# Backward start of an attention and MLP block: a V tile and a dK tile exchanged, the rows of e released by an earlier add, dw4 stored in two parts

## The chip, the cores and the metric

The kernel runs on one core of one Trainium2 chip. The metric is the device time of one execution in microseconds (us), lower is better. Engines are named as in the profile: PE is TensorE, PEld its weight loads, DVE is VectorE, ACT is ScalarE, POOL is GpSimd and SP is SyncE; SP and POOL here mostly issue transfers, SP the loads and POOL the stores.

## The reference

One decode step of an adaptive-layernorm block and its gradients. The sizes are D = 640, 32 heads, 8192 cached positions, 192 columns per head, F = 1536, all arrays bf16.

```python
mod = (silu(c) @ w_mod).reshape(1, 6, 1, -1)          # sa, ca, ga, sb, cb, gb
h = layernorm(x) * (1 + ca) + sa
q = (h @ wq)                                          # 32 heads of 192
p = softmax(q K^T * 192 ** -0.5)                      # K: 32 x 8192 x 192
x = x + ga * ((p V) @ wo)
h = layernorm(x) * (1 + cb) + sb
x1 = h + shift_mix(h)                                 # one position: the mixed part is zero
out = x + gb * (x1 + gelu(layernorm(x1) @ w3) @ w4)
# returned: out and its gradients for x, K, V, wq, wo, w3, w4, c, w_mod
```

The large arrays are K and V, each 32 x 8192 x 192 numbers. Both are read, and dK and dV of the same size are written. For one head, dV is the outer product of the row of probabilities with do (the gradient of that head's output), and dK is the outer product of the column dS with q, where dS = p * (V do - correction). V is therefore read a second time in the backward part, to form V do.

## The kernel before, in words

**Tiles.** A head's K or V is handled in two halves of 128 partitions x 32 rows x 192 columns, 1536 KB each. Five such tiles, `KB0` to `KB4`, hold halves of K in the forward part; three, `VB[0]` to `VB[2]`, hold halves of V. Lines 353 and 354 give the five KB tiles names by their use at the end of the forward part, and the order `OB` in which the backward part uses them for its outputs:

```python
KX, KY, KC, KD, KE = (KB[(2 * HQ + k) % NKB] for k in (-4, -5, -3, -2, -1))
OB = (KC, KY, KX, KE, KD)
```

So KX is KB0, KC is KB1, KD is KB2, KE is KB3 and KY is KB4.

**The forward loop** (lines 516 to 600) goes over heads 0 to 30; the last head is finished by straight-line code from line 605 on. The last half of V goes to KY (line 665). KX then takes rows 4 to 11 of w4 (`load_rows`, lines 730 and 765), and KC takes part of the transposed w3 and of the transposed wo.

**The middle** (lines 731 to 975) finishes the attention output, runs the MLP forward and its gradients, and ends in `dao`, the gradient of the attention output. The pieces that the change names are these:
- `mp_out` (line 443) copies head 30's sums from PSUM on ACT, the second copy to the tile `mt`; `m_add` (line 456) adds that tile to a half of PSUM on DVE. Before, they stand at lines 910 and 954.
- `dw4_dve` (line 877) and `dw4_act` (line 912) each make some of the 12 row blocks of the gradient of w4, 128 x 640 per block, on DVE or ACT; `dw4_store` (line 881) issues their store on POOL. Before, blocks 0 and 1 are made at line 933, ahead of the product `pr` (line 935) that leads to `dao_bf` (line 952); blocks 2 and 3 follow at line 955, with a store of four blocks from KX. Blocks 4 to 8 go to KX too (lines 1353 to 1355), blocks 9 to 11 to the staging tile `stg0` (lines 1356 and 1357), each with a store of its own.
- `dx1_out` and `d_sb_out` (lines 958 and 968) are small vector computations, kept together with that of `du` in the list `late0` (line 1362).

**The backward loop** (line 1363) has 64 steps. Step s works on half `ht(s)`: step 0 on the second half of head 31 (V in KY), step 1 on its first half (V in `VB[2]`), steps 2 and 3 on head 30 (V in `VB[0]` and `VB[1]`), and so on downwards. For each half,
- `mul_q(s, 0)` and `mul_q(s, 1)` (line 1036) multiply V by do on DVE, a half of the half at a time; `tree_q` (line 1051) sums the products over the columns on PE with an identity matrix, into the one PSUM tile `dot_ps`; `dot_sum` (line 343) finishes the sum on DVE, as `dP`;
- `dv_groups` (line 1058) forms dV: PE multiplies a row of e (tile `er_b`, loaded by `load_er` from a scratch array in DRAM) with do into `dv_ps`, and ACT copies the result into the dV tile;
- `dk_part` (line 1070) forms dK on DVE from q and dS;
- `dv_store` and `dk_store` (lines 1316 and 1320) issue the stores on POOL; `load_v` (line 324) issues the load of the V half four steps on, on SP.

The start of step 0 is written out ahead of the loop (lines 1324 to 1362). The list `OL` gives dV and dK of successive steps the tiles of `OB` in turn: dV of step 0 KC, dK of step 0 KY, dV of step 1 KX, dK of step 1 KE, dV of step 2 KD, dK of step 2 KC, dV of step 3 KY. `v_buf(s)` gives the tile of V: KY for step 0, `VB[2]`, `VB[0]`, `VB[1]` for steps 1 to 3, and then these three in turn. V of step 4 thus goes to `VB[2]`, and its load, issued within step 0 (line 1407), waits for `mul_q(1, 1)`.

**What sets the order.** Within the forward and the backward part the program order is kept on PE, DVE, ACT and SP; POOL's stores are issued in program order too. A transfer into a tile waits for the last reader of the tile, and a write to a tile waits for the stores that read it. The pools of the backward part (`bst`, from line 982) lie over space that the forward part's pools held, and what is placed there waits for the last use of what lay there before: the two loads of `er_b` on line 1029 wait for the add in `m_add` that reads `mt`, and for the last matmul of line 919.

Besides the halves, `slot()` (line 1282) hands out side work (gradients of wo, wq, w3, w_mod and the output vectors) over the steps, by a count of slots that does not depend on time.

Of the kernel before, what the change touches and what calls it, by code (L numbers as in the profile page):

```python
# [20 lines left out]
def kernel(  # L21
# [28 lines left out]
    D = A_x.shape[-1]  # L50
# [66 lines left out]
    def tcol(n, name, dtype=FP32):  # L117
        return tmp.tile([P, n], dtype, name=name)
# [7 lines left out]
    def mean_sum(ps, groups, name):  # L126
        m = tcol(groups, name)
        V_.reduce_sum(out=m, in_=ps[:, 0 : groups * ND].rearrange("p (a b) -> p a b", b=ND), axis=AX.X)
        return m
# [187 lines left out]
    def flat(kb):  # L317
        return kb.rearrange("p j d -> p (j d)")


    NVB = 3
    VB = [vp.tile([P, JH, DH], BF16, name=f"VB{b}") for b in range(NVB)]

    def load_v(h, t, v):
        nc.sync.dma_start(out=v, in_=V_hd[h][:, t * JH : (t + 1) * JH, :])
        return v
# [24 lines left out]
    H1 = HQ - 1  # L351
    TL = NT - 1
    KX, KY, KC, KD, KE = (KB[(2 * HQ + k) % NKB] for k in (-4, -5, -3, -2, -1))
    OB = (KC, KY, KX, KE, KD)
    NVA = (7 * JQ) // 16
    MO = 256
    with tc.tile_pool(name="vs", bufs=3) as vsp, tc.tile_pool(name="ft", bufs=2) as ft, \
# [85 lines left out]
        def mp_out(h, mp):  # L443
            A_.copy(out=M1[:, h, :], in_=mp[:, 0:MW])
            mt = ft.tile([P, MW], FP32, name="mt", bufs=1)
            A_.copy(out=mt[64:128, :], in_=mp[64:128, MO : MO + MW])
            return mt

        def m_out(h, mp, op, os_):
            mt = mp_out(h, mp)  # L450
            o, z_h = os_head(h, os_)
            A_.copy(out=o, in_=op[:, 0:DH])
            A_.copy(out=z_h, in_=op[:, DH:MW])
            return mt

        def m_add(h, mp, mt):
            t, b = divmod(h, 2)
            V_.tensor_tensor(out=M2[64 * b : 64 * b + 64, t, :], in0=mp[0:64, MO : MO + MW], in1=mt[64:128, :], op=ALU.add)
# [56 lines left out]
        with tc.manual_schedule(engines=ORDER):  # L515
            for i in range(H1):
# [34 lines left out]
                if z is not None:  # L551
                    mt = m_out(i - 2, z["mp"], z["op"], os_)
# [124 lines left out]
            mt = m_out(H1 - 2, z["mp"], z["op"], os_)  # L677
# [15 lines left out]
            mp = psM.tile([P, 512], FP32, name="mp")  # L693
# [119 lines left out]
            def w3t(n=1):  # L813
                for _ in range(n):
                    next(w3t_it, None)
# [56 lines left out]
            w3t()  # L872
            pe.pop(0)()
            w3t()
            dw4_v = out_7.rearrange("(a p) r -> p a r", p=P)

            def dw4_dve(dst, a0, lo, hi):
                for a in range(lo, hi):
                    V_.tensor_scalar(out=dst[:, (a - a0) * D : (a - a0 + 1) * D], in0=dbo_bc, scalar1=g_[:, a : a + 1], scalar2=None, op0=ALU.mult)

            def dw4_store(dst, lo, n):
                nc.gpsimd.dma_start(out=dw4_v[:, lo : lo + n, :], in_=dst[:, 0 : n * D].rearrange("p (a r) -> p a r", a=n))
# [24 lines left out]
                    T_.matmul(h2_ps[:, k : k + 1], lhsT=w4r(a)[:, k * P : (k + 1) * P], rhs=g_bf[:, a : a + 1], start=(a == 0), stop=(a == NF - 1))  # L907
            do_t(TL, 0)
            do_t(TL, 8)
            mt = mp_out(H1 - 1, mp)  # L910

            def dw4_act(dst, a0, lo, hi):
                for a in range(lo, hi):
                    A_.activation(out=dst[:, (a - a0) * D : (a - a0 + 1) * D], in_=dbo_bc, func=ACT.Copy, scale=g_[:, a : a + 1])

            dn_ps = psO.tile([P, 256], FP32, name="dn_ps", tag="op")[:, 0:ND]
            for k in range(ND):
                for a in range(NF):
                    T_.matmul(dn_ps[:, k : k + 1], lhsT=w3T(a, k), rhs=du_bf[:, a : a + 1], start=(a == 0), stop=(a == NF - 1))

            sk = mean_sum(ps5, 5, "sk")
            w6 = col(6 * ND, "w6").rearrange("p (a b) -> p a b", b=ND)
            A1, Ag, B1, Bg, uu, vv = (w6[:, k, :] for k in range(6))
# [6 lines left out]
            NWg = col(4 * ND, "NWg").rearrange("p (a b) -> p a b", b=ND)  # L930
            V_.tensor_scalar(out=NW, in0=NW, scalar1=rho[:, 0:1], scalar2=None, op0=ALU.mult)
            V_.tensor_copy(out=bo, in_=h2_ps[:, 0:ND])
            dw4_dve(flat(KX), 0, 0, 2)
            pr = col(4 * ND, "pr").rearrange("p (a b) -> p a b", b=ND)
            V_.tensor_tensor(out=pr, in0=dn_ps[:, None, :].to_broadcast([P, 4, ND]), in1=G, op=ALU.mult)
            ps = mean_mm(pr.rearrange("p a b -> p (a b)"), 4 * ND)
# [14 lines left out]
            V_.reduce_sum(out=qr, in_=q4.rearrange("p a b -> p b a"), axis=AX.X)  # L951
            V_.tensor_tensor(out=dao_bf, in0=vg, in1=qr, op=ALU.add)
            V_.tensor_copy(out=d_n2, in_=dn_ps)
            m_add(H1 - 1, mp, mt)
            dw4_dve(flat(KX), 0, 2, 4)
            dw4_store(flat(KX), 0, 4)

            def dx1_out():
                q = pr
# [28 lines left out]
    NS = 2 * HQ  # L988
# [9 lines left out]
    def ht(s):  # L998

        return H1 - s // 2, (1 - s % 2 if s < 2 else s % 2)  # L1000
# [7 lines left out]
    stg0 = bst.tile([P, ND * CW], BF16, name="stg")  # L1008
# [38 lines left out]
    def half_q(s, q):  # L1047
        if halved(s, q):
            V_.tensor_tensor(out=pq[:, q, :, 0:HW], in0=pq[:, q, :, 0:HW], in1=pq[:, q, :, HW:DH], op=ALU.add)
# [8 lines left out]
    def dv_groups(dV, er, doh, gs):  # L1058

        dV4 = dV.rearrange("p (r k) d -> p r (k d)", r=4)  # L1060
        for g in gs:
            m, q = divmod(g, 2)
            ps = psV.tile([P, 2, 512], FP32, name="dv_ps", tag="v")
            for k in range(2):
                for b in range(2):
                    p0 = 32 * (2 * q + b)
                    T_.matmul(ps[:, b, k * DH : (k + 1) * DH], lhsT=er[p0 : p0 + 1, 2 * m + k, :], rhs=doh[p0 : p0 + 1, :], start=True, stop=True)  # L1067
            A_.copy(out=dV4[:, 2 * q : 2 * q + 2, m * PW : (m + 1) * PW], in_=ps[:, :, 0:PW])  # L1068
# [219 lines left out]
            prog[1] += 1  # L1288

    def v_buf(s):  # L1290
        return KY if s == 0 else VB[(s + 1) % NVB]

    OL = [OB[i % 5] for i in range(2 * NS - 5)]
    OL += [v_buf(NS - 3), OB[3], v_buf(NS - 2), OB[4], v_buf(NS - 1)]
    v_l = {s: v_buf(s) for s in range(4)}
# [27 lines left out]

    dV0 = OB[0]
    er = er_l.pop(0)
# [5 lines left out]
    do_mm(TL, 0)  # L1331
    mul_q(0, 1)
    half_q(0, 1)
    dv_groups(dV0, er, doh, (4,))
    tree_q(ps, 0, 0, 0, 6)
    dv_groups(dV0, er, doh, (6,))
# [13 lines left out]
    T_.matmul(c_ps, lhsT=c32, rhs=cs, start=True, stop=True)  # L1350
    dv_groups(dV0, er, doh, (5, 7))
    dv_store(0, dV0, JQ, JH)
    dw4_dve(flat(KX)[:, 4 * D :], 4, 4, 7)
    dw4_act(flat(KX)[:, 4 * D :], 4, 7, 9)
    dw4_store(flat(KX)[:, 4 * D :], 4, 5)
    dw4_act(stg0[:, 2 * D :], 9, 9, 12)
    dw4_store(stg0[:, 2 * D :], 9, 3)
    V_.scalar_tensor_tensor(out=cpr, in0=c_ps, scalar=32.0, in1=rinv, op0=ALU.mult, op1=ALU.mult)
    V_.memset(dha, 0.0)
    V_.memset(dsc, 0.0)  # L1360
# [1 line left out]
    late0 = [lambda: V_.scalar_tensor_tensor(out=du, in0=t_, scalar=-1.0, in1=d_g, op0=ALU.mult, op1=ALU.mult), dx1_out, d_sb_out]  # L1362
    for s in range(NS):
        h, t = ht(s)
        nxt = s + 1 < NS
        doh = do_of(h)
        qh = qs_bc[:, h * DH : (h + 1) * DH]
        dP = tcol(JH, "dP")
        dot_sum(ps, dP)
        dS4 = bst.tile([P, JH, 4], BF16, name="dS4", bufs=2)  # L1370
        V_.scalar_tensor_tensor(
            out=dS4,
            in0=dP[:, :, None].to_broadcast([P, JH, 4]),
            scalar=cpr[:, h : h + 1],
            in1=E_all[:, h, t * JH : (t + 1) * JH, None].to_broadcast([P, JH, 4]),
            op0=ALU.subtract,
            op1=ALU.mult,
        )
        dV, dK = OL[2 * s], OL[2 * s + 1]
        gs = [0, 1, 2, 3, 4, 5, 6, 7]  # L1380
        if not nxt:
            gs = [0, 2, 4, 6, 1, 3, 5, 7]
        if s == 0:
            gs = [None] * 8
        else:
            er = er_l.pop(s)
        if nxt:
            ps = psR.tile([P, JH, TS], FP32, name="dot_ps")

        def dv(k):  # L1390
            if gs[k] is not None:
                dv_groups(dV, er, doh, (gs[k],))

        def tree(q, lo, hi):
            if nxt:
                tree_q(ps, s + 1, q, lo, hi)

        dv(0)
        dv(1)
        slot()  # L1400
        tree(0, 0, 4)
        if nxt:
            mul_q(s + 1, 1)
            half_q(s + 1, 1)
            v_l.pop(s + 1, None)
        if s + 4 < NS:
            v_l[s + 4] = load_v(*ht(s + 4), v_buf(s + 4))
        dv(2)
        tree(0, 4, 8)
        dv(3)  # L1410
        tree(0, 8, 12)
        if row is not None:
            dq_cols(row)
            row = None
        dk_part(dK, qh, dS4, 0, JQ)
        if not nxt:
            dv_store(s, dV, 0, JQ, nc.sync)
            dk_store(s, dK, 0, JQ)
        slot()
        dv(4)  # L1420
        tree(1, 0, 3)
        dk_part(dK, qh, dS4, JQ, JH)
        while late0:
            late0.pop(0)()
        dk_store(s, dK, 0 if nxt else JQ, JH)
        dv(5)
        tree(1, 3, 6)
        slot()
        dv(6)
        tree(1, 6, 9)  # L1430
        dv(7)
        if s + 2 < NS:
            er_l[s + 2] = load_er(s + 2)
        if s == 0:
            pass
        elif nxt:
            dv_store(s, dV, 0, JH)
        else:
            dv_store(s, dV, JQ, JH, nc.sync)
        tree(1, 9, 12)  # L1440
        if h == H1:
            row = dq_rows(t, (KD, KE)[t], dS4)
        if s + 2 < NS:
            assert (s + 2) // 4 in done
            mul_q(s + 2, 0)
            half_q(s + 2, 0)
        done_s[0] = s + 1
        slot()
# [33 lines left out]
```

## Time and profile before

| what | us |
|---|---|
| three runs | 1411.46, 1413.57, 1414.79 |
| median | 1413.57 |
| the profiled execution | 1412.54 |
| its span, from the first to the last instruction | 1410.8 |
| busy in the span: PE | 1182.7 |
| DVE | 1112.0 |
| ACT | 902.5 |
| POOL | 106.0 |

1.74 us of the profiled execution lie outside its span. It moved 569.36 MB in its transfers, 404 GB/s over the span. The loads of V and K and the stores of dV and dK are 1536 KB each: 64 loads of K, 123 loads of V under that name (and more under others), 123 stores from the KB tiles. In the profile's pages, a line of the timeline gives the start in us, the busy time, engine, source line, operation, what is written and read, and, in brackets, the engine's idle time before it and what ended it. A line of the table of windows gives, for a stretch of the span, its length, the busy time of PE, PEld, DVE, ACT and POOL with the number of instructions in parentheses, the clock granted to PE as a share of full speed, the mean busy share of the core's 16 DMA engines, and the GB/s that they moved. That share is of packets in flight and can pass 1 by a little.

### The profile page before, as it was taken

The page shows a single profiled execution, that of the slowest core. Times are in us where ns is not written, and L with a number is a line of the kernel's source. Part 1 is how long each engine was busy: PE and PEld are TensorE (multiplying, and loading weights), DVE is VectorE, ACT ScalarE, POOL GpSimd, SP SyncE. Part 2 cuts the span into 40 slices and gives each one's busy share as a digit, 9 for nine tenths or more (in the row PEclk, how much of TensorE's full clock was granted, in tenths as well). Part 3 has the DMA queues.
Part 4 walks back from the last instruction along what each step waited for, and adds up shares of the span by engine and source line. Part 5 has one row for each costly group of instructions (what it writes and reads, how often), then busy time and mean ns, then how long its engine had stood idle before and what let it go on. Part 6 is the DMA issues. An engine that isn't in the chain of part 4 may idle for free.

```text
span 1410.8 us, 30413 instructions
## 1 busy us (share of the span) xinstructions
PE 1182.7 (84%) x12680; PEld 745.5 (53%) x12680; DVE 1112.0 (79%) x1461; ACT 902.5 (64%) x1971; POOL 106.0 (8%) x191
## 2 busy tenths in 40 slices
PE   3988989999998999797867998896877799878965
PEld 2777777777777778443323444443443344334421
DVE  4989999999999998886755875776775777868765
ACT  0767777777777778565545666665655476546654
POOL 0000000000000000110100111101110111101110
PEclk7899999999999999665555555556556555555555
DMA  9999999999999997599999999999999999999998
GB/s 375 389 398 419 418 416 423 411 422 417 418 415 415 408 416 291 209 365 427 424 388 424 427 422 426 421 425 425 425 421 425 414 413 426 419 404 396 424 369 373
DMA packets 76200, 569.36 MB, mean 404 GB/s; under 512 B 7294, under 2 KB 25038, under 8 KB 35998
## 3 DMA queue, kind: packets, MB, share of 16 engines
q1 hardware_dynamic: 51162, 342.03, 59.4%
q0 software_dynamic: 24384, 224.87, 38.3%
q8 instruction: 99, 1.62, 0.4%
q10 hardware_dynamic: 516, 0.51, 0.1%
q14 instruction: 39, 0.32, 0.1%
HBM read 340.95 MB, written 226.43 MB: 402 GB/s over the span
## 4 chain that ended last, share of the span: by engine, by line
issue 58%; DMA 17%; PE 9%; DVE 9%; POOL 5%; ACT 1%; SPq 0%; POOLq 0%; DVEq 0%; ACTq 0%
DMA KB<-in_A_k_cache_dram 7%; DVE prod L330 4%; DMA out_dram<-KB 3%; DMA w_st<-in_A_wq_dram 3%; PE mp L402 2%; DVE prod L334 2%; PE dot_ps L1056 2%; POOL out_dram L1322 2%; POOL out_dram L1318 2%; DMA out_dram<-w_st 2%; DMA stg<-in_A_wq_dram 2%; PE half_ps L340 2%; DMA out_dram<-stg 1%; PE mp L407 1%; PE dv_ps L1067 1%
## 5 line engine op out<-in xcount | busy, mean ns | idle before, releaser
L1068 ACT CAST KB<-dv_ps 128x768 bf16<-128x768 f32 x512 | 397.5, 805 | 164.1 <-PE dv_ps L1067 156.6
L1056 PE MATMUL dot_ps<-pq,ident_bf 128*128 128x256 bf16 x1494 | 380.3, 398 | 22.5 <-DVE dP L344 20.2
L1072 DVE TENSOR_TENSOR KB<-qs_bc,dS 128x3072 bf16<-128x3072 bf16 x122 | 210.7, 1753 | 131.8 <-DMA out_dram<-KB 124.6
L387 ACT ACTIVATE vs<-VB,Ef 128x192 bf16<-128x192 bf16 x840 | 303.5, 447 | 0.0
L1056 PEld LDWEIGHTS <-ident_bf 128*128 128x128 bf16 x1494 | 150.4, 124 | 177.6 <-issue 137.8
L1067 PE MATMUL dv_ps<-do_r,er_b 1*128 1x192 bf16 x2048 | 231.1, 337 | 9.5 <-ACT KB L1068 6.5
L1037 DVE TENSOR_TENSOR pq<-VB,do_r 128x3072 bf16<-128x3072 bf16 x126 | 220.4, 1749 | 15.4 <-PE dot_ps L1056 15.4
L330 DVE TENSOR_TENSOR prod<-KB,qs_bc 128x6144 bf16<-128x6144 bf16 x62 | 207.9, 3353 | 25.5 <-DMA KB<-in_A_k_cache_dram 19.8
L402 PE MATMUL mp<-vs,KB 128*128 128x193 bf16 x1984 | 191.2, 249 | 4.2 <-ACT vs L387 3.3
L402 PEld LDWEIGHTS <-KB 128*128 128x128 bf16 x1984 | 170.4, 98 | 13.3 <-DMA KB<-in_A_k_cache_dram 5.3
L894 ACT COPY wT<-wT_ps 128x1024 bf16<-128x1024 bf16 x82 | 79.1, 965 | 120.4 <-PE wT_ps L893 115.5
L1067 PEld LDWEIGHTS <-er_b 1*128 1x128 bf16 x2048 | 69.6, 104 | 161.1 <-issue 157.9
L340 PE MATMUL half_ps<-prod,ident_bf 128*128 128x256 bf16 x744 | 95.1, 279 | 44.2 <-DVE prod L334 44.1
L380 DVE TENSOR_TENSOR vs<-VB,E 128x1728 bf16<-128x1728 bf16 x120 | 123.7, 1052 | 0.3 <-ACT vs L387 0.3
L334 DVE TENSOR_TENSOR prod<-prod 128x3072 bf16<-128x3072 bf16 x62 | 108.7, 1754 | 1.0
L407 PE MATMUL mp<-vs,KB 128*64 128x193 bf16 x1976 | 107.2, 252 | 0.0
L340 PEld LDWEIGHTS <-ident_bf 128*128 128x128 bf16 x744 | 72.9, 100 | 62.4 <-issue 53.4
L344 DVE TENSOR_REDUCE dP<-dot_ps 128x32 f32<-128x512 f32 x64 | 44.0, 687 | 59.7 <-PE dot_ps L1056 59.5
L407 PEld LDWEIGHTS <-KB 128*64 128x64 bf16 x1976 | 80.1, 110 | 20.1 <-issue 19.7
L367 ACT ACTIVATE E<-S_h,negm 128x256 bf16<-128x256 f32 x31 | 15.8, 508 | 114.9 <-DVE negm L538 112.6
L1322 POOL DMA_DIRECT2D out_dram<-KB x61 | 33.6, 551 | 488.2 <-DVE KB L1072 300.4
L422 PE MATMUL op<-vs,ones_bf 128*32 128x193 bf16 x1920 | 62.1, 250 | 0.0
(359 smaller groups left out, 972.0 us busy)
## 6 DMA issues: line engine op xcount, KB each, us to landing
VB<-in_A_v_cache_dram SPq DMA_DIRECT2D x123, 1536.0 KB
out_dram<-KB POOLq DMA_DIRECT2D x123, 1536.0 KB, 16.1
KB<-in_A_k_cache_dram SPq DMA_DIRECT2D x64, 1536.0 KB
wo_st<-in_A_wo_dram SPq DMA_DIRECT2D x31, 480.0 KB
w_st<-in_A_wq_dram SPq DMA_DIRECT2D x12, 960.0 KB
out_dram<-wo_st POOLq DMA_DIRECT2D x16, 480.0 KB, 16.3
out_dram<-w_st POOLq DMA_DIRECT2D x7, 960.0 KB, 20.6
w_st<-in_w_mod_dram SPq DMA_DIRECT2D x6, 960.0 KB
```

The lines of the kernel that those rows point to most:

```text
L330: V_.tensor_tensor(out=prod, in0=src, in1=vec[:, None, :].to_broadcast([P, JH, DH]), op=ALU.mult)
L334: V_.tensor_tensor(out=prod[:, :, 0:HW], in0=prod[:, :, 0:HW], in1=prod[:, :, DH - HW : DH], op=ALU.add)
L340: T_.matmul(ps, lhsT=ident_bf, rhs=prod[:, :, k : k + TF], start=(k == 0), stop=(k == w - TF))
L380: V_.tensor_tensor(out=vs[:, 0:n, 0:DH].rearrange("p j (a b) -> p j a b", b=4), in0=v[:, v0 : v0 + n, :].rearrange("p j (a b) -> p j a b", ...
L387: A_.activation(out=vs[:, k, 0:DH], in_=v[:, v0 + k, :], func=ACT.Copy, scale=Ef[:, j0 + k : j0 + k + 1])
L402: T_.matmul(mp[:, 0:MW], lhsT=kb[:, j0 + k, 0:P], rhs=vs[:, k, 0:MW], start=(q == 0 and k == 0), stop=(z and k == JQ - 1), skip_group_chec ...
L407: T_.matmul(mp[p0 : p0 + 64, MO : MO + MW], lhsT=kb[:, j0 + k, P:DH], rhs=vs[:, k, 0:MW], start=False, stop=(z and k >= JQ - 2), skip_grou ...
L1037: V_.tensor_tensor(out=pq[:, q], in0=v_l[s][:, q * JQ : (q + 1) * JQ, :], in1=do_of(ht(s)[0])[:, None, :].to_broadcast([P, JQ, DH]), op=AL ...
L1056: T_.matmul(ps[:, q * JQ : (q + 1) * JQ, :], lhsT=ident_bf, rhs=pq[:, q, :, k : k + TS], start=(k == 0), stop=(k == w - TS), skip_group_ch ...
L1067: T_.matmul(ps[:, b, k * DH : (k + 1) * DH], lhsT=er[p0 : p0 + 1, 2 * m + k, :], rhs=doh[p0 : p0 + 1, :], start=True, stop=True)
L1068: A_.copy(out=dV4[:, 2 * q : 2 * q + 2, m * PW : (m + 1) * PW], in_=ps[:, :, 0:PW])
L1072: V_.tensor_tensor(out=dK[:, lo:hi, :].rearrange("p j (a b) -> p j a b", b=4), in0=qh.rearrange("p (a b) -> p a b", b=4)[:, None, :, :].to ...
```

## The change

Five edits, all between the end of the forward part and step 3 of the backward loop.
- `OB` has `VB[2]` in the place of KY, and `v_buf` has KY in the place of `VB[2]` from step 4 on. V of step 4 goes to the tile of V of step 0, and dK of step 0 to the tile of V of step 1. The load for step 4 is issued right after `half_q(0, 1)`, ahead of the loop.
- `mp_out` and `m_add` of head 30 move up: the copies ahead of the transposes of wo (`do_t`), the add ahead of `sk`.
- dw4: three blocks instead of two ahead of `pr`, three more behind `dao_bf`, all six in KX with one store; the other six on ACT in `stg0` with one store. DVE makes 6 blocks instead of 7, ACT 6 instead of 5, and there are two stores instead of three.
- The three entries of `late0` are taken one at a time in steps 1, 2 and 3, instead of all in step 0.
- The last steps use the same list with the two tiles exchanged.

```diff
-    OB = (KC, KY, KX, KE, KD)
+    OB = (KC, VB[2], KX, KE, KD)
...
+            mt = mp_out(H1 - 1, mp)
             dw4_v = out_7.rearrange("(a p) r -> p a r", p=P)
...
             do_t(TL, 0)
             do_t(TL, 8)
-            mt = mp_out(H1 - 1, mp)
...
+            m_add(H1 - 1, mp, mt)
             sk = mean_sum(ps5, 5, "sk")
...
             V_.tensor_copy(out=bo, in_=h2_ps[:, 0:ND])
-            dw4_dve(flat(KX), 0, 0, 2)
+            dw4_dve(flat(KX), 0, 0, 3)
...
             V_.tensor_copy(out=d_n2, in_=dn_ps)
-            m_add(H1 - 1, mp, mt)
-            dw4_dve(flat(KX), 0, 2, 4)
-            dw4_store(flat(KX), 0, 4)
+            dw4_dve(flat(KX), 0, 3, 6)
+            dw4_store(flat(KX), 0, 6)
...
     def v_buf(s):
-        return KY if s == 0 else VB[(s + 1) % NVB]
+        return KY if s == 0 else VB[2] if s == 1 else (VB[1], KY, VB[0])[s % 3]
...
     half_q(0, 1)
+    v_l[4] = load_v(*ht(4), v_buf(4))
     dv_groups(dV0, er, doh, (4,))
...
     dv_store(0, dV0, JQ, JH)
-    dw4_dve(flat(KX)[:, 4 * D :], 4, 4, 7)
-    dw4_act(flat(KX)[:, 4 * D :], 4, 7, 9)
-    dw4_store(flat(KX)[:, 4 * D :], 4, 5)
-    dw4_act(stg0[:, 2 * D :], 9, 9, 12)
-    dw4_store(stg0[:, 2 * D :], 9, 3)
+    dw4_act(stg0, 6, 6, 12)
+    dw4_store(stg0, 6, 6)
...
-        if s + 4 < NS:
+        if 0 < s < NS - 4:
             v_l[s + 4] = load_v(*ht(s + 4), v_buf(s + 4))
...
-        while late0:
+        if s > 0 and late0:
             late0.pop(0)()
         dk_store(s, dK, 0 if nxt else JQ, JH)
```

## The prediction

> **What bounds the kernel now.** First the page: the span, and the row of DMA shares in its 40 slices of 35.3 us.
>
> ```profile
> span 1410.8 us, 30413 instructions
> ...
> DMA  9999999999999997599999999999999999999998
> ```
>
> The DMA engines are full nearly throughout. Only slices 15 and 16, some 529 to 600 us, fall: the turn from forward to backward. A table of windows says how much, and what follows (the last columns are PE's clock, DMA share, GB/s):
>
> ```profile
> 574.00:608.00 34.00, 26.98 (x223) 15.35 (x224) 27.48 (x43) 18.62 (x27) 4.41 (x7) 0.55 0.74 285
> 608.00:640.00 32.00, 29.30 (x205) 12.74 (x205) 25.28 (x25) 22.89 (x32) 3.75 (x7) 0.66 0.99 382
> 640.00:700.00 60.00, 48.31 (x312) 21.33 (x313) 41.63 (x51) 34.46 (x48) 7.15 (x13) 0.56 1.01 426
> 700.00:1340.00 640.00, 531.25 (x3914) 257.56 (x3910) 451.36 (x684) 383.48 (x513) 72.26 (x125) 0.54 1.01 418
> ```
>
> From 608 us on no engine is full but DMA is, so the bytes left decide: a change earns what DMA time it fills ahead of that, 34 x (1 - 0.74) = 8.8 us at most after 574 us (what is idle before 574 us it doesn't touch). Windows of 2 us show where these 8.8 us lie:
>
> ```profile
> 574.00:576.00 2.00, 0.86 (x9) 0.59 (x10) 1.97 (x3) 0.33 (x1) 0.00 (x0) 0.50 0.79 284
> 576.00:578.00 2.00, 2.00 (x14) 0.89 (x14) 1.97 (x3) 2.00 (x4) 0.00 (x0) 0.50 0.14 49
> 578.00:580.00 2.00, 2.00 (x14) 0.81 (x14) 1.93 (x5) 1.27 (x3) 0.38 (x1) 0.50 0.00 0
> ...
> 582.00:584.00 2.00, 1.73 (x14) 1.04 (x11) 1.96 (x7) 1.64 (x3) 0.00 (x0) 0.50 0.29 114
> 584.00:586.00 2.00, 2.00 (x11) 1.44 (x10) 2.00 (x2) 2.00 (x4) 0.95 (x2) 0.50 0.42 173
> ...
> 590.00:592.00 2.00, 0.00 (x0) 0.00 (x0) 2.00 (x4) 0.34 (x1) 0.00 (x0) 1.00 0.90 268
> ...
> 602.00:604.00 2.00, 2.00 (x17) 1.31 (x16) 2.00 (x2) 1.30 (x3) 0.38 (x1) 0.50 0.48 203
> ```
>
> Two holes: 576 to 586 us, and 602 to 605 us. The timeline names who would have filled them:
>
> ```profile
> 572.25 1.14 SPq L995 DMA_DIRECT2D er_b<-eT_d  x2
> ...
> 575.13 0.82 PE L1067 MATMUL dv_ps<-do_r,er_b 1*128 1x192 bf16 x8 [2.37 <-DVE pq L1037]
> ...
> 584.93 44.26 SPq L325 DMA_DIRECT2D VB<-in_A_v_cache_dram  x5
> ...
> 590.09 1.75 DVE L1037 TENSOR_TENSOR pq<-VB,do_r 128x3072 bf16<-128x3072 bf16 x1
> ...
> 596.65 2.24 ACT L1068 CAST KB<-dv_ps 128x768 bf16<-128x768 f32 x3 [6.32 <-DMA out_dram<-KB]
> ...
> 603.62 0.55 POOL L1322 DMA_DIRECT2D out_dram<-KB  x1 [14.50 <-DVE KB L1072]
> ...
> 645.81 1.76 DVE L1072 TENSOR_TENSOR KB<-qs_bc,dS 128x3072 bf16<-128x3072 bf16 x1 [7.63 <-DMA out_dram<-KB]
> ```
>
> V of step 4 is asked for at 584.93 us. ACT stands 6.32 us before the first dV of step 1, until the second dw4 store has left KX; so dK of step 1 goes out only at 603.62 us: the second hole. By 645.81 us DVE itself waits 7.63 us for a store: compute is ahead of DMA.
>
> **The change part by part.** All times are on the axis of the profiled execution.
>
> *The add and dw4, ahead of `dao_bf`.* The add takes 0.39 us of DVE's line (571.83 to the next start at 572.22), and its `mt` will be ready some 0.1 us after 567.53 us, where `sk` starts now. The third dw4 block adds 0.33 us (three take 0.97 at 581.15). Together 0.84 us, of which DVE's wait of 0.57 us for `dn_ps` ahead of `pr` hides all but 0.27. `do_r`, now ready at 573.23 us, comes at 573.5. Were that wait gone, the cost would be 0.84. On ACT the two copies of `mp_out` (0.66 us) go into its idle 1.23 us ahead of the wo transposes at 568.07.
>
> *Rows of e.* Their loads are held by the add (ends 572.18) and by the last `dn_ps` matmul (ends 569.9); only the second is left, so they go 2.3 us sooner. First use followed the issue by 575.13 - 572.25 = 2.9 us; from 569.95 that is 572.8, so the first dV matmul then waits for `do_r`: 573.5, 1.6 us sooner. PE soon meets DVE again: the products of the second quarter are done at 578.68 (+0.27), and the sums that lead to `c_ps` start at 579.0 instead of 579.60. So 0.57 us are kept.
>
> *dw4 blocks out of step 0.* Three blocks (0.97 us, 581.15 to 582.12) leave DVE just ahead of `cpr`, which then follows `c_ps`: the 0.57 us pass on. `mul_q(1, 1)` starts at 582.6 instead of 583.15, dK of step 0 is ready at 587.7 instead of 588.24.
>
> *`late0`.* Twelve small operations, 588.16 to 590.09 = 1.93 us, leave step 0, so `mul_q(2, 0)` starts at 587.6 instead of 590.09. They come back as 0.2, 0.9 and 0.9 us in steps 1 to 3, where DMA is full (below) and covers them.
>
> *The store from KX.* Six blocks go out at some 573.4 us (now 573.19 with four, moved within 2.1 us of it), so they have landed by 578 and ACT's 6.32 us go. PE's 2.66 us at 594.84 (its next matmul is at 597.50) go with them. PE starts step 1 at 590.0 instead of 592.50; the second product of step 1 ends at 592.0 instead of 594.5, and V of step 5 is asked for then. `dq_x` comes 2.5 + 2.66 = 5.1 us sooner, and so the dK store of step 1: 598.5 instead of 603.62.
>
> *ACT's blocks, ahead of the dK store.* Six instead of five, 0.76 each (2.26 for 3): done at some 588.0 instead of 587.45. POOL issues in order, so the dK store of step 0 waits for their store: 589.1 instead of 588.54, a loss of 0.6, within the second hole below.
>
> *V of step 4.* It waits for the product that ends now at 575.93 + 1.75 = 577.68, so 578.0 instead of 584.93. SP has nothing else to issue between; V of step 5, next behind it, waits for a later product anyway. 1536 KB (1.573 MB) at the 425 GB/s of the full windows are 3.7 us.
>
> *Sum, by DMA time.* From the issue on POOL at 579.62 to the rise of DMA in the window from 580 us it is about 1.0 us; for a load from SP I take 1.5 (bounds 0.5 and 2.9, the latter the rows of e). After the change DMA carries: dw4, 0.98 MB, 574.3 to 577.2 (the present four blocks: 0.79 + 0.14 of 2 us = 1.86 us for 0.666 MB); idle 2.3; V of step 4 with the first half of dV 0 from 579.5, 2.36 MB, 5.5 us, to 585.0; the second half (issue 583.9) to 586.9; idle 2.3, until dw4's second store (issue 588.2) starts at 589.2; then dw4 2.8, dK 3.7 and V of step 5 3.7 us, to 599.4, when dK of step 1 (598.5 + 1.0) is there, and dV and V 6 behind it. By 608 us the present kernel has moved 34 us x 285 GB/s = 9.69 MB: dw4 (1.97), dV and dK of step 0 and V of steps 4 and 5 (4 x 1.573), and 1.43 MB of that dK; the new one has done this at 599.5 + 3.4 = 602.9 to 603.7. So 4.3 to 5.1 us, of which I take 4.4, because the dK of step 2 (616.26, 5.1 sooner) may find DMA dry for part of a microsecond. Bounds: with the SP latency at its worst and 2 us dry after step 1, 1.5 us; with neither hole, 8.8.
>
> 1412.54 - 4.4 = 1408.1. The profiled execution lies 1.03 us under the median of the runs, so the median forecast is **1409**.
>
> Two rules of the Trainium skill bear on this. PE's clock is 0.50 in the windows from 572 to 588 us, though PE is busy in them, and 1.00 at 590. The page "TensorE: Matmul & The Clock Gate" (Part 1, "What's actually happening") has activity of about 3.4 us release the half-rate clock, and idle time bring it back. By that, PE without its two stops stays fast through steps 1 and 2; the estimate would be up to 1 us lower, as dK of step 2 is then not late. The trace had 12 busy microseconds at 0.50 first, so I don't count on it. And the page "DMA: Bandwidth & Descriptors" ("Specifications") gives line rate from 512 B on, while the dw4 store, rows of 1280 B, made 0.666 MB in 1.86 us, 358 GB/s, against 425: by the page two blocks in idle time are worth 0.77 us, by the row 0.92.
>
> **The rivals.**
> *The gain is given back.* DMA runs dry again behind step 1, because the small operations of steps 1 to 3 (2.0 us) and a lost stretch of full clock delay compute. The windows from 610 to 618 us have clock 1.00; at 0.50 a step's 24 sums and 8 dV groups cost 24 x 0.108 + 8 x 0.16 = 3.9 us more (four sums take 0.60 against 1.03, a group 0.34 against 0.50). 5.1 - 2.0 - 3.9 is under zero, some 3 us of DMA: 1412. Against it: DMA has a backlog then.
> *Both holes close.* If V of step 4 flows within 0.5 us and the other times fall well, 7 us: 1406. Against it: nothing is there to send between 587 and 589 us.
> *Slower: both queues stop at once.* At 1348 to 1356 us DMA falls to 0.77 and 0.48 while POOL waits 17.7 us for DVE and SP for DVE's product, DVE itself 9.94 us for a store: 0.23 x 4 + 0.52 x 4 = 3.0 us lost. A w tile's store (line 1162) stands with dK there. The shifted phase could do it at three more such points: 9 - 4.4 = 4.6 slower, 1418. It decides from the second. Against it: the profile has many such points, and loses so much at one.
> *The loads of e aren't sooner* (another holder): it costs 0.57 us at most and stays within the forecast.
>
> **How the numbers follow.** The forecast (1407 to 1410.7, alone) has 0.64, both holes closed 0.06, given back 0.17, slower 0.13. The bound of 0.2% is 2.8 us, about what a measurement can tell: under 1410.7 is faster, over 1416.4 slower. Faster 0.70, same 0.17, slower 0.13. The range 1404.5 to 1414 leaves out the slower case and a little of the low one.
>
> **What would show it.** ACT's wait at 596.65 gone; a V load near 578; dK of step 1 near 598.5; the DMA share between 574 and 608 at 0.86 or more, and the stretch behind it as full as now. Wrong, if DMA falls under 0.95 between 608 and 640, or if a later stage holds new idle time.

## The result, and the profile after

| | before | after |
|---|---|---|
| median of 7 runs, us | 1413.57 | 1405.56 |
| from lowest to highest | 1409.40 to 1415.95 | 1403.17 to 1409.52 |
| the profiled execution | 1412.54 | 1404.99 |
| its span | 1410.8 | 1403.2 |

The ratio is 0.9955, with a 95% interval of 0.9939 to 0.9972: 4.0 to 8.6 us faster, 6.4 in the middle. A second comparison, told below, gave 0.9966 (0.9955 to 0.9977), 4.8 us. The forecast was 4.4 us less and 1409.

The page of the changed kernel, its span and the row of DMA shares in 40 slices:

```profile
span 1403.2 us, 30406 instructions
...
DMA  9999999999999997699999999999999999999998
```

Slice 16 (561 to 596 us) has gone from 5 to 6 and the rest is as it was. The table of windows for the same stretches as in the prediction (the last three columns are PE's clock, the DMA share and GB/s):

```profile
574.00:608.00 34.00, 30.98 (x260) 17.74 (x257) 27.32 (x33) 23.15 (x34) 3.54 (x6) 0.60 0.93 348
608.00:640.00 32.00, 30.19 (x190) 11.67 (x189) 25.03 (x32) 21.23 (x28) 3.74 (x7) 0.50 0.99 394
640.00:700.00 60.00, 52.12 (x320) 22.65 (x315) 44.53 (x57) 36.28 (x50) 8.98 (x16) 0.50 1.01 424
700.00:1340.00 640.00, 528.63 (x3918) 257.26 (x3918) 446.80 (x679) 381.35 (x512) 70.22 (x122) 0.54 1.01 418
```

The share between 574 and 608 us has risen from 0.74 to 0.93, and behind it DMA is as full as before. The timeline of the changed kernel answers to the lines shown of the kernel before:

```profile
568.40 1.12 SPq L995 DMA_DIRECT2D er_b<-eT_d  x2
...
572.06 0.82 PE L1067 MATMUL dv_ps<-do_r,er_b 1*128 1x192 bf16 x8 [0.51 <-ACT do_r L1021]
...
576.49 0.34 SPq L325 DMA_DIRECT2D KB<-in_A_v_cache_dram  x1
...
587.49 1.50 ACT L1068 CAST KB<-dv_ps 128x768 bf16<-128x768 f32 x2
...
595.73 0.53 POOL L1322 DMA_DIRECT2D out_dram<-KB  x1 [8.02 <-DVE KB L1072]
...
605.10 0.16 DVE L1313 TENSOR_TENSOR dq_x<-dq_c,dq_x 128x1 f32<-128x1 f32 x1 [4.26 <-PE dq_c L1312]
```

The rows of e and V of step 4 are asked for sooner, ACT makes the first dV of step 1 with no wait ahead of it, and dK of step 1 goes out at 595.73 us. The two axes can't be laid on each other as they are: the store of the rows of e, which no edit touches, was issued at 560.76 us in the execution before and at 559.33 in this one. All 14 profiled executions of this study, of 13 kernels that are alike up to there, have it between 558.87 and 561.49. **From here on, instants with a plus sign are counted from that store.** On that axis dK of step 1 goes from +42.9 to +36.4, 6.5 us sooner, and dK of step 2 from +55.5 to +50.2. The span ends at +843.9 instead of +850.0, so some 6 of the 7.6 us between the two executions lie behind the mark.

The best measure of the turn is what DMA moved from +10 to +90 us. The window of the kernel before, then that of the changed kernel:

```profile
570.76:650.76 80.00, 64.57 (x481) 32.12 (x482) 60.40 (x81) 48.38 (x67) 9.98 (x17) 0.59 0.85 332
```

```profile
569.33:649.33 80.00, 71.74 (x506) 35.25 (x506) 62.12 (x81) 51.18 (x70) 9.17 (x16) 0.54 0.92 359
```

80 us at 332 and 359 GB/s are 26.6 and 28.7 MB. The 2.16 MB between them take 5.1 us at the 425 GB/s of the full windows.

### The profile page after: what moved, and what is told of

Its sections match the earlier page's. It is cut to its first block, busy times and chain, and to the rows that moved or that the text cites. A ratio compares the mean times of both kernels' runs of the same rounds, so it can differ in the third digit from the quotient of the medians.

```text
span 1403.2 us, 30406 instructions
## 1 busy us (share of the span) xinstructions
PE 1182.8 (84%) x12680; PEld 744.5 (53%) x12680; DVE 1111.0 (79%) x1460; ACT 903.2 (64%) x1972; POOL 104.9 (7%) x190
## 4 chain that ended last, share of the span: by engine, by line
issue 42%; DVE 21%; DMA 17%; PE 11%; POOL 5%; ACT 1%; SPq 0%; POOLq 0%; DVEq 0%
DMA KB<-in_A_k_cache_dram 10%; DVE prod L330 8%; DVE prod L334 4%; PE mp L402 3%; DMA out_dram<-KB 3%; DVE vs L380 2%; POOL out_dram L1322 2%; PE half_ps L340 2%; POOL out_dram L1318 2%; DMA w_st<-in_A_wq_dram 2%; PE mp L407 2%; DVE pq L1037 2%; DMA wo_st<-in_A_wo_dram 1%; PE dot_ps L1056 1%; DMA out_dram<-VB 1%
## 5 line engine op out<-in xcount | busy, mean ns | idle before, releaser
L1068 ACT CAST KB<-dv_ps 128x768 bf16<-128x768 f32 x416 | 321.5, 803 | 108.6 <-PE dv_ps L1067 106.3
L1072 DVE TENSOR_TENSOR KB<-qs_bc,dS 128x3072 bf16<-128x3072 bf16 x98 | 169.4, 1753 | 103.5 <-DMA out_dram<-KB 91.8
L1037 DVE TENSOR_TENSOR pq<-VB,do_r 128x3072 bf16<-128x3072 bf16 x86 | 150.5, 1749 | 12.7 <-PE dot_ps L1056 12.7
L1068 ACT CAST VB<-dv_ps 128x768 bf16<-128x768 f32 x96 | 75.1, 802 | 39.3 <-PE dv_ps L1067 39.1
L1072 DVE TENSOR_TENSOR VB<-qs_bc,dS 128x3072 bf16<-128x3072 bf16 x30 | 51.5, 1753 | 29.5 <-DMA out_dram<-VB 24.8
```

The costliest lines, as they stand in the source:

```text
L1037: V_.tensor_tensor(out=pq[:, q], in0=v_l[s][:, q * JQ : (q + 1) * JQ, :], in1=do_of(ht(s)[0])[:, None, :].to_broadcast([P, JQ, DH]), op=AL ...
L1072: V_.tensor_tensor(out=dK[:, lo:hi, :].rearrange("p j (a b) -> p j a b", b=4), in0=qh.rearrange("p (a b) -> p a b", b=4)[:, None, :, :].to ...
```

## The experiments

Eleven more kernels and the changed one again, each timed beside the kernel before (6 to 12 runs of each). Names with u_ are the changed kernel with one edit undone, names with d_ the kernel before with some edits done, names with v_ the changed kernel with something added. All compute the whole of the reference. The measurements together, ordered by dK of step 2:

| kernel | ratio (95% interval) | dK of step 1 out | of step 2 | MB, +10 to +90 |
|---|---|---|---|---|
| before | 1 | +42.9 | +55.5 | 26.6 |
| d_late | 1.0009 (0.9997 to 1.0022) | +42.5 | +55.2 | 26.6 |
| u_late | 0.9975 (0.9963 to 0.9987) | +39.5 | +54.1 | 27.0 |
| d_ring | 0.9991 (0.9979 to 1.0004) | +40.2 | +54.0 | 27.1 |
| d_dw4 | 0.9989 (0.9979 to 1.0000) | +40.1 | +53.3 | 27.6 |
| u_dw4 | 0.9965 (0.9952 to 0.9978) | +37.9 | +51.0 | 28.5 |
| d_dl | 0.9969 (0.9955 to 0.9983) | +36.9 | +50.6 | 28.5 |
| u_add | 0.9952 (0.9935 to 0.9969) | +37.8 | +50.5 | 28.6 |
| after | 0.9955 (0.9939 to 0.9972) | +36.4 | +50.2 | 28.7 |
| a_again | 0.9966 (0.9955 to 0.9977) | +36.4 | +50.1 | 28.8 |
| v_five | 0.9954 (0.9939 to 0.9968) | +37.1 | +50.1 | 28.8 |
| u_ring | 0.9959 (0.9943 to 0.9975) | +36.2 | +48.6 | 29.3 |
| v_dq | 0.9966 (0.9953 to 0.9979) | +34.8 | +47.7 | 29.5 |
| v_both | 0.9944 (0.9928 to 0.9960) | +34.8 | +47.7 | 29.6 |

Every kernel whose dK of step 2 goes out after +53 has a ratio of 0.9975 or more; every one where it goes out before +51.1 has 0.9969 or less. Within the second group, from 28.5 to 29.6 MB, the ratios show no order that the intervals can tell.

**One edit undone at a time.** The ring:

```diff
-    OB = (KC, VB[2], KX, KE, KD)
+    OB = (KC, KY, KX, KE, KD)
-        return KY if s == 0 else VB[2] if s == 1 else (VB[1], KY, VB[0])[s % 3]
+        return KY if s == 0 else VB[(s + 1) % NVB]
-    v_l[4] = load_v(*ht(4), v_buf(4))
-        if 0 < s < NS - 4:
+        if s + 4 < NS:
```

> The changed kernel with the old tile ring alone: V of step 4 in VB[2] again, asked for after the second product of step 1. Times are counted from the store of the rows of e (eT_d); in the window from 10 to 50 us after it DMA was idle 12.0 us before and 6.0 us after the change. The DMA-time theory (the gain is the DMA time filled before 608 us): the load moves from 17.2 to about 23.5, DMA is idle there for about 2 us more (8 in all), dK of step 1 still goes out near 36.4, and the kernel takes about 2 us more than the changed one, 1407.5. The compute-chain theory (the gain is the earlier compute, by ACT's wait that is gone and the small operations moved; V of step 4 is needed much later): the time stays that of the changed kernel, 1405.6.

Measured: the load at +23.5 as expected, idle DMA time from +10 to +50 of 8.8 us instead of 6.0, and yet a ratio of 0.9959, the changed kernel's. The DMA-time theory is not borne out as it was put: V of step 4 in the first hole filled 2.8 us of idle time and bought no time that this measurement can tell. The intervals leave some 3 us either way, so by the time alone the 2 us of that theory are not excluded; the bytes speak against it too. The windows from +50 to +70 show where the lead was lost. The changed kernel:

```profile
609.33:619.33 10.00, 8.75 (x57) 3.49 (x53) 9.79 (x18) 6.28 (x10) 2.11 (x4) 0.50 0.96 379
619.33:629.33 10.00, 9.58 (x60) 3.64 (x60) 9.57 (x9) 6.67 (x9) 1.10 (x3) 0.50 1.00 369
```

The same stretch with the old ring:

```profile
609.81:619.81 10.00, 8.57 (x50) 3.26 (x52) 9.86 (x16) 5.40 (x7) 1.08 (x2) 0.50 1.01 426
619.81:629.81 10.00, 9.58 (x64) 3.71 (x64) 8.47 (x8) 6.36 (x9) 1.09 (x3) 0.50 1.02 429
```

Both have a busy share near 1, but the changed kernel moves 7.5 MB there and the other 8.6. At +50 the early load was 0.5 MB ahead; at +90 it is 0.6 MB behind. A part of this can be PE's clock: with the old ring it was 0.84 on average from +40 to +50 (0.67 in the changed kernel), DVE's wait at `dq_x` in step 2 was 2.85 us instead of 4.26, and dK of step 2 went out 1.6 us sooner. One execution of each can't part the two.

dw4, with the lines of the kernel before in the place of the new ones:

```diff
-            dw4_dve(flat(KX), 0, 0, 3)
+            dw4_dve(flat(KX), 0, 0, 2)
...
-            dw4_dve(flat(KX), 0, 3, 6)
-            dw4_store(flat(KX), 0, 6)
+            dw4_dve(flat(KX), 0, 2, 4)
+            dw4_store(flat(KX), 0, 4)
...
-    dw4_act(stg0, 6, 6, 12)
-    dw4_store(stg0, 6, 6)
+    dw4_dve(flat(KX)[:, 4 * D :], 4, 4, 7)
+    dw4_act(flat(KX)[:, 4 * D :], 4, 7, 9)
+    dw4_store(flat(KX)[:, 4 * D :], 4, 5)
+    dw4_act(stg0[:, 2 * D :], 9, 9, 12)
+    dw4_store(stg0[:, 2 * D :], 9, 3)
```

> The changed kernel with dw4 alone as before: 2 and 2 blocks, 5 more in KX, 3 in the staging tile, three stores. ACT then stands before the first dV of step 1 until the store has left KX. Both theories: dK of step 1 goes out near 42 (36.4 in the changed kernel, 42.9 before) from the e store. DMA-time theory: V of step 4 still fills the first hole, the second one is back for some 2.5 us: idle 8.5 us, 1408. Compute-chain theory: steps 1 and on are 5 us later and so is all: 1410.5.

Measured: 0.9965, no more than 1.4 us over the changed kernel's two ratios, where the theories had 2.4 and 4.9, with dK of step 1 at +37.9. Both were wrong on the wait. The timeline of ACT, where the first dV of step 1 goes to KX, which dw4's second store again reads:

```profile
589.66 0.80 ACT L1068 CAST KB<-dv_ps 128x768 bf16<-128x768 f32 x1
591.09 1.60 ACT L1068 CAST KB<-dv_ps 128x768 bf16<-128x768 f32 x2 [0.63 <-DMA out_dram<-KB]
```

0.63 us are left of 6.32, with dw4 as before. So dw4's grouping alone did not make KX late; what stood ahead of its store did. In the kernel before, V of step 4 was asked for at 584.93 us and dw4's second store at 585.59. Its DMA view, queue by queue (q1 holds SP's loads, q0 POOL's stores; packets, MB, share), first from 587 to 592 us and then from 592 to 596:

```profile
q1 hardware_dynamic: 112, 1.38, 86.3%
q0 software_dynamic: 37, 0.12, 11.0%
...
q0 software_dynamic: 291, 1.44, 87.6%
q1 hardware_dynamic: 32, 0.20, 12.2%
```

The load's packets went first for five microseconds, and the store's hardly at all; then it turned round. What the view calls a packet is one row of V here (1.38 MB / 112 = 12.3 KB). The Trainium skill, page "DMA: Bandwidth & Descriptors" ("Queues, rings and completion order"), says that a DMA engine takes turns between its queues by whole packets of some 9 to 17 descriptors. A half of V is 128 rows of 12288 B, 8 for each of 16 engines; with one descriptor for a row, a whole load would by that rule pass in one turn (an estimate). The trace agrees for this load, as load and stores took turns and did not share the time evenly.

> The changed kernel with the small operations (late0) all in step 0 again. The second product's first half of step 2 starts 1.9 us later and dK of step 1 goes out near 38.3 instead of 36.4. DMA-time theory: dw4, dK of step 0 and V of step 5 are still in flight until then, idle grows by 0 to 0.8 us, time within 1 us of the changed kernel's. Compute-chain theory: 1.9 us more, 1407.5.

```diff
-        if s > 0 and late0:
+        while late0:
```

The time is 1.3 to 2.8 us over the changed kernel's (0.9975 against its two ratios), nearer to the compute-chain theory; the intervals overlap, and the same edit makes 2.8 us between d_dw4 and d_dl below. But dK of step 1 goes out 3.1 us later than in the changed kernel, which is more than either theory had. Two rows of windows show why, each of them 3.4 us long, the steps in which the clock column changes. The changed kernel, with PE's first sums of step 1 behind them:

```profile
586.73:590.15 3.42, 2.43 (x45) 1.35 (x38) 3.38 (x4) 2.54 (x4) 0.98 (x2) 1.00 0.76 262
590.15:593.56 3.41, 3.41 (x23) 2.33 (x23) 2.19 (x4) 1.77 (x4) 0.00 (x0) 0.50 1.15 434
```

```profile
588.45 0.60 PE L1056 MATMUL dot_ps<-pq,ident_bf 128*128 128x256 bf16 x4 [0.99 <-DVE dP L344]
```

And the same of u_late:

```profile
585.27:588.68 3.41, 1.32 (x42) 0.84 (x41) 3.20 (x14) 2.09 (x4) 1.38 (x2) 1.00 0.70 255
588.68:592.09 3.41, 2.15 (x12) 0.96 (x11) 3.23 (x4) 0.67 (x1) 0.00 (x0) 0.50 1.08 426
```

```profile
589.94 1.01 PE L1056 MATMUL dot_ps<-pq,ident_bf 128*128 128x256 bf16 x4 [3.35 <-DVE dP L344]
```

PE has full clock for one such stretch at this place. In the changed kernel PE works 2.43 us of it, and the stretch reaches into the sums of step 1, whose first four take 0.60 us. With the small operations ahead of `dP`, PE waits 3.35 us for it instead of 0.99, works 1.32 us of the fast stretch, and the first four sums take 1.01 us at half clock. They start at +31.07 instead of +29.12: 1.95 us, which is the small operations' own time. The rest is in DVE's wait for PE ahead of dK of step 1, in the changed kernel and in u_late:

```profile
591.64 0.16 DVE L1313 TENSOR_TENSOR dq_x<-dq_c,dq_x 128x1 f32<-128x1 f32 x1 [1.18 <-PE dq_c L1312]
```

```profile
594.31 0.16 DVE L1313 TENSOR_TENSOR dq_x<-dq_c,dq_x 128x1 f32<-128x1 f32 x1 [2.37 <-PE dq_c L1312]
```

That is 1.19 us more, and 1.95 + 1.19 = 3.1 us, as measured. The pair d_dl and d_dw4, below, has the same two waits (1.18 and 2.37 us) and the same first sums (0.60 and 1.01 us). This is read from the traces; no run here sets the clock.

> The changed kernel with the add of head 30 where it was, behind dao_bf. The rows of e are loaded 2.3 us later. By the prediction that is worth 0.57 us at most to the chain: dK of step 1 near 37.0 (36.4 in the changed kernel), time within 0.6 us of it, 0.9960 to 0.9968 to the kernel before. If the first dV is what sets the chain: 1.6 us more, 0.9972.

```diff
-            mt = mp_out(H1 - 1, mp)
...
             do_t(TL, 8)
+            mt = mp_out(H1 - 1, mp)
...
-            m_add(H1 - 1, mp, mt)
             sk = mean_sum(ps5, 5, "sk")
...
             V_.tensor_copy(out=d_n2, in_=dn_ps)
+            m_add(H1 - 1, mp, mt)
```

The rows of e were asked for at +11.5 instead of +9.1, dK of step 1 went out at +37.8 (1.4 us later, where 0.6 was expected), but dK of step 2 at +50.5 and the ratio of 0.9952 show no loss. In time the early add is worth nothing that can be told; the intervals leave some 3 us either way.

**Edits done alone.** The kernel before with the ring:

> The kernel before with the new tile ring and the early V load alone. Theory of two ways to one gain (V of step 4, asked for at 24.2, stood in the DMA queues ahead of dw4's second store at 24.8, so that KX came free late; loading V earlier or storing dw4 otherwise both end that wait): ACT's wait of 6.32 us before the first dV of step 1 falls under 2 us with no edit of dw4; dK of step 1 goes out near 40.4 (42.9 before; 37.9 without the dw4 edit alone, and 1.9 and 0.6 for the two other edits), time 3 to 4 us under the kernel before, 0.9975. Theory of the prediction, by which that wait is dw4's own: the wait stays 5 us or more, dK of step 1 stays near 42.9, V of step 4 fills the first hole alone: 2 us, 0.9985.

The kernel before with dw4 regrouped:

> The kernel before with dw4 regrouped alone. Both theories: ACT's wait of 6.32 us is gone, and dK of step 1 goes out near 38.7 (36.2 with the other two edits, 1.9 and 0.6 later without). Theory of two ways to one gain: time 3 to 4 us under the kernel before, 0.9975, as much as by the ring alone. DMA-time theory: idle time in the first hole stays, the second closes: 2.5 us, 0.998.

ACT's first dV of step 1 with the ring alone, then with dw4 alone:

```profile
589.55 0.80 ACT L1068 CAST KB<-dv_ps 128x768 bf16<-128x768 f32 x1 [0.38 <-DMA out_dram<-KB]
```

```profile
588.45 1.50 ACT L1068 CAST KB<-dv_ps 128x768 bf16<-128x768 f32 x2
```

Each alone takes ACT's wait away (0.38 us is left with the ring) and brings dK of step 1 to +40.2 and +40.1: 2.7 to 2.8 us sooner, nearly the same (38.7 had been expected of dw4). The two edits are two ways to one gain. In time they make only 1.3 and 1.5 us, nearer to the 2 and 2.5 of the theories beside it than to the 3 to 4 of this one, and with intervals that reach to no gain: with `late0` still in step 0, dK of step 2 comes at +54.0 and +53.3. `late0` spread alone (the one line above, the other way round):

> The kernel before with the small operations (late0) spread over steps 1 to 3, alone. Arrival theory (what counts is when dK of steps 1 and 2 are ready, which needs every hold on the way taken off; times from the e store): ACT's wait for KX is there as before, since V of step 4 still goes ahead of dw4's second store, so dK of step 1 stays within 1 us of 42.9 and the time within 1 us of the kernel before, ratio 0.9995 to 1.0005. If the operations count by themselves: 1.9 us, 0.9986.

The ratio is 1.0009, no gain, close to what the arrival theory had. The wait is in its place:

```profile
597.02 2.24 ACT L1068 CAST KB<-dv_ps 128x768 bf16<-128x768 f32 x3 [6.17 <-DMA out_dram<-KB]
```

Then dw4 and `late0` together, without ring, early load and early add:

> The kernel before with dw4 regrouped and late0 spread, without the new ring, the early V load and the early add. Arrival theory: dK of step 1 near 36.8, of step 2 near 50, so nearly the whole gain: 4 to 5 us, 0.9967. If the edits add up as single gains (dw4 alone made 1.5 us, late0 undone cost 1.3 to 2.9): 2.8 to 4.4 us, 0.9974.

0.9969, with dK of steps 1 and 2 at +36.9 and +50.6, and 28.5 MB: nearly the whole gain. 1.5 us from dw4 and -1.3 from `late0` make 4.4 together. The arrival theory stands between the kernel before and the changed one: it was put after d_dw4 and d_ring had been measured, and what it said of d_late and d_dl came so. Adding up single gains does not: 1.5 - 1.3 = 0.2 us lies under the interval of d_dl (2.4 to 6.4 us). The sum as it was put, with u_late in the place of d_late, has 4.4 us as its upper end, which that interval doesn't exclude.

**The changed kernel again, and what could be had on top.**

> The changed kernel unaltered, beside the kernels it is compared with here. Every theory: ratio 0.995 to 0.996 to the kernel before. It also shows what one execution differs from another: idle DMA time from 10 to 90 us after the e store within 0.5 us of 6.4, dK of step 2 near 50.2, if PE's full-clock stretches fall as in the first execution; up to 2 us sooner or later if they don't.

The turn of this execution is a copy of the first one's: dK at +36.4 and +50.1, 28.8 MB, the clock in the same stretches. So for this kernel, the only one with two profiles, the table's last three columns hardly differ between two executions. The ratio, 0.9966, a little over what was expected, shows what scatter the time has.

A timeline line shown above gives the next wait: DVE stands 4.26 us at `dq_x` in step 2, for two products that PE has behind twelve sums. Put behind dK:

```diff
-        if row is not None:
-            dq_cols(row)
-            row = None
         dk_part(dK, qh, dS4, 0, JQ)
...
         dk_part(dK, qh, dS4, JQ, JH)
+        if row is not None:
+            dq_cols(row)
+            row = None
```

> The changed kernel with the two small adds of dq (and their products on PE) behind dK in each of the first steps, instead of ahead of it. DVE waits for these products for 1.2 us in step 1 and 4.3 us in step 2 there. If compute still sets the time behind 608 us: dK of step 1 goes out near 35, dK of step 2 near 46 instead of 50.2, the last dip of the DMA share (0.88 in 50 to 54) closes, and the kernel takes 1 to 3 us less, 1404. If DMA has a backlog there, as the prediction had it, the stores only queue up sooner: 1405.6.

dK goes out at +34.8 and +47.7, and 0.8 MB more have been moved at +90, but the ratio is that of a_again beside it, 0.9966, as the second theory had it: DMA has a backlog there. So beyond the changed kernel an earlier dK alone gains nothing that can be told. V of step 5 sooner:

```diff
+    OB = (KC, KX, KE, VB[0], KD)
+        return KY if s == 0 else VB[2] if s == 1 else VB[0] if s == 2 else (VB[1], KY, VB[2])[s % 3]
...
+        if s == 0:
+            v_l[5] = load_v(*ht(5), v_buf(5))
+        elif 1 < s < NS - 4:
```

> The changed kernel with another ring: dK of step 0 in KX, dV of step 1 in KE, dK of step 1 in VB[0], and V of step 5 in VB[2], asked for right after the second product of step 1 (near 23.5 from the e store instead of 31.2). DMA-time theory: the hole before dw4's second store (idle 1.0 us) closes, idle 5 us instead of 6.0, 1404.5. Compute-chain theory: nothing on the engines is sooner, the time is that of the changed kernel, 1405.6.

DMA has no idle time left from +20 to +30, but 1.0 us of it from +30 to +40, because dK of step 1 came at +37.1: the hole moved by 10 us, and the time stayed. Both together:

> The changed kernel with both additions, V of step 5 into VB[2] right after step 1's second product, and the adds of dq behind dK. Alone the first had no idle DMA time left from 20 to 30 us but 1.0 us of it from 30 to 40, as dK of step 1 (37.1) came too late; the second had dK of step 1 at 34.8 and idle time from 20 to 30. If the bytes moved early are kept: 90 us after the e store 29.7 MB or more (28.7 in the changed kernel, 29.5 with the second alone), and 1.5 to 2 us less than the changed kernel, 0.9950. If what is gained there is lost behind, as in each of the two alone: 0.9962, as the changed kernel.

```profile
569.85:649.85 80.00, 71.54 (x526) 35.56 (x525) 63.44 (x82) 52.84 (x74) 9.17 (x16) 0.58 0.94 370
```

29.6 MB, and 0.9944 is the lowest ratio of all, 7.9 us under the kernel before. Whether it beats the changed kernel is not settled: its interval overlaps both of that kernel's, and the two were timed in different comparisons.

## Why the prediction was right

The time, 1405.56, lies in the range of 1404.5 to 1414, and the forecast of 4.4 us lies inside both intervals (4.0 to 8.6, and 3.2 to 6.4). By its steps:

- *What bounds the kernel.* Right in the main: from +70 to +780 the DMA share is 1.00 or 1.01 in all 14 executions, and the kernels that moved 28.5 MB or more by +90 have the lower ratios (0.9944 to 0.9969, against 0.9975 to 1.0009). What it lacks is that a share near 1 does not tell the rate (below), so that "what DMA time it fills" is no measure of the gain.
- *The add and dw4 ahead of `dao_bf`, rows of e.* Right in the trace: the loads are 2.4 us sooner. `mul_q(1, 1)` starts at +21.7 instead of +22.4. But this is worth nothing in time that can be told (u_add).
- *The store from KX.* Right that ACT's 6.32 us go, and right in size: "PE's 2.66 us" was credited, and taking only this wait away moved dK of step 1 by 2.7 us. What was missing is its cause, which stood in the shown lines: V of step 4 at 584.93 us, just ahead of the store. So the prediction credited one wait to dw4 alone where the early load removes it too; for this wait one of the two edits would have done.
- *ACT's blocks.* For the dK store of step 0 "a loss of 0.6" was put down. It did not come: the store goes out at +27.8 before and after.
- *`late0`.* The mis-sized term: "Twelve small operations, 588.16 to 590.09 = 1.93 us" were taken at their duration. They cost 3.1 us on dK of step 1 (u_late; d_dl against d_dw4 gives 3.2), since PE's one full-clock stretch then passes ahead of the sums. That is most of the difference between the 6.5 us by which dK of step 1 is sooner and the 5.1 that had been worked out. Whether the gain in time is above the forecast, the intervals can't tell.
- *V of step 4.* The load came within 1.5 us of the forecast instant (576.49 against 578.0, 1.43 of it the shift of the whole execution). The step that failed is "1536 KB (1.573 MB) at the 425 GB/s of the full windows are 3.7 us" as a gain: the load filled the hole, at 273 to 301 GB/s, and later windows moved less. Undone, it costs nothing that can be told.
- *The sum.* "4.3 to 5.1 us, of which I take 4.4" was made with two terms of which one (the early load, beside the other edits) brought nothing that can be told and the other (the arrival of dK) brought more. The bytes give 5.1. That the two errors offset is luck; the method, what DMA has moved at a fixed point, held.
- *Rivals.* The gain is not given back behind step 1, though the condition of that rival came true: from 608 to 640 us PE's clock is 0.50 throughout, where it was 0.66. DMA still has a share of 0.99 there; 0.88 in the window from 609 to 613 us is the only dip. Both holes did not close, as 6.0 us are idle from +10 to +50 (12.0 before). The slower case did not come; the dip that it rests on has moved by some 8 us with the change and has not grown (0.63 at 1348 to 1356 us before, 0.75 at 1340 to 1348 after, and 0.68 there in a_again).
- *The clock rule.* The prediction gave up to 1 us less by it. Those stretches did not stay fast (below), so the result under 1409 is no support for it.

## What to carry to other kernels

When two buffers' transfers share the DMA engines, a wait for a store can be due to the load asked for just ahead of it: look up what was issued in the microsecond before, since moving either one ends the wait, and doing both pays once. Where several holds lie on one way, single edits show little or nothing (1.3, 1.5 and -1.3 us here) and two of them together nearly all (4.4); so test pairs before an edit is dropped. Count the bytes moved by a fixed time after a fixed event, not idle time filled: 2.8 us of filled idle time bought nothing here that could be told. How far the lessons reach beyond this kernel no run here shows.

## What the runs showed of the hardware

- A busy share near 1 is not full speed. The load of V of step 4 alone made 273 GB/s with a share of 1.05 in the changed kernel:

```profile
580.00:582.00 2.00, 1.72 (x14) 1.02 (x9) 1.96 (x7) 1.77 (x3) 0.00 (x0) 0.50 1.05 273
```

As nearly the only transfer from 587 to 592 us before, it made 300 GB/s. In the windows at 425 GB/s loads run beside stores. But loads alone are not always slow: from 200 to 300 us, in the forward part of the changed kernel, SP's queue had 99.8% of the share at 416 GB/s. Stores alone made 431 GB/s from 584 to 586 us. What makes the difference stays open.

- PE's clock in the changed kernel is full, from 586 us on, only in stretches of 3.4 us or two of them in a row, with 13 us or more at half between, though PE is busy. From the end of one fast stretch to the end of the next:

```profile
590.15:603.77 13.62, 13.59 (x108) 7.45 (x108) 8.52 (x10) 8.93 (x14) 1.07 (x2) 0.50 1.01 391
603.77:607.19 3.42, 2.97 (x28) 1.73 (x28) 2.04 (x3) 1.97 (x4) 0.00 (x0) 1.00 1.00 422
```

PE is busy 13.59 of 13.62 us, the clock is 0.50, and only then does it rise for 3.42 us. The Trainium skill, page "TensorE: Matmul & The Clock Gate" (Part 1, "What's actually happening"), has 3.4 us of activity raise it; by that it would have risen at 593.56. The measurement decides; what grants the stretches stays open.
